# The last quarter of the attention output projection, taken into the next gated layer as seven products for each pair of tiles

## The chip, the core and the metric

The kernel runs on one core of one Trainium2 chip. A core has five engines with a queue each: TensorE (PE) for matrix products, VectorE (DVE), ScalarE (ACT), GpSimd (POOL), and SyncE (SP), which here only starts transfers. TensorE writes its results to PSUM (here in banks of 128 x 512 float32 words), from which VectorE and ScalarE read them; everything else is in SBUF. The metric is the device time of one launch in microseconds, and the median of several launches counts.

## What is computed

Four layers act in turn on x, 2048 tokens of 1024 bfloat16 values: linear attention, gated layer, and both once more with the same weights.

```python
def _A_ref(x, wqkv, wo):                     # 32 heads of 32
    q, k, v = heads of x @ wqkv
    phi = lambda t: jnp.where(t > 0, t + 1, jnp.exp(t)) + 1e-6
    pq, pk = phi(q), phi(k)
    kv = jnp.einsum("bhsd,bhse->bhde", pk, v)
    z = jnp.einsum("bhsd->bhd", pk)
    num = jnp.einsum("bhqd,bhde->bhqe", pq, kv)
    den = jnp.einsum("bhqd,bhd->bhq", pq, z)[..., None] + 1e-6
    return (num / den) @ wo
def _B_ref(x, W_gate, W_up, W_down):         # 1024 -> 3584 -> 1024
    gate, up = x @ W_gate, x @ W_up
    return (gate * (gate > 0) * up) @ W_down
x = x + _A_ref(_layernorm(x), wqkv, wo)
x = x + _B_ref(_layernorm(x), W_gate, W_up, W_down)
x = x + _A_ref(_layernorm(x), wqkv, wo)
x = x + _B_ref(_layernorm(x), W_gate, W_up, W_down)
```

## The kernel before

**Tiles.** The 2048 tokens are 16 tiles of 128 (x0 to x15), four tiles are a quarter (`sc` or `q`, 0 to 3), and the first eight tiles are the "first half" (`NS` = 8). x stays in SBUF as float32. Layers 0 and 2 are attention (`layer_A`), layers 1 and 3 are gated (`layer_B`).

**Attention, second part.** When the sums over all tokens are there, the product of the keys and values is multiplied into the output weights (`fold_wo`), which gives two slots T of 128 x 4 x 1024 in bfloat16. The output of a tile is then `out_unit` (lines 627 to 639): for each half of 512 columns, eight matmuls of the tile's transposed queries `pqT` by T, and one VectorE addition of the PSUM bank onto x (line 638). Before that, each tile's queries go through `z_mult`, `z_sum` and `z_scale` (lines 586 to 605; POOL, VectorE, POOL) and a DMA transpose into `pqT`. `out0` are the eight units of quarter 0, column by column; the loop of line 709 then runs eight units each for the quarters 1, 2 and 3, tile by tile.

**Norms for the gated layer.** `ln_later` and `ln_at` set four steps for a tile: `ln_norm` (two BATCH_NORM_STATS and one aggregate on VectorE, then Ln and Exp on ScalarE), the scaled copy `xnb` in float16 on ScalarE (line 188), a DMA transpose into `xnT` on SP's queue (line 352), and, for each pair of tiles, four VectorE sums `sums_x` (lines 796 to 799). Before the change the tiles 0 to 3 are normed while quarter 1's units run, and the tiles 4 to 7 while quarter 2's run; quarter 3's eight units come last, ahead of the first gated unit.

**The gated layer.** `glu` (line 807) does one of 14 units `u` for each half of the tokens (`c` = 0, 1). It uses Strassen's scheme in Winograd's form: a product of two by two blocks takes seven block products, not eight. For the gate (`g`) and the up projection (`u`) each there are products 5, 1, 2, 6, 7, 3, 4 of four matmuls, 56 in a unit. Products 5, 6, 7 and 3 use `sums_x`; products 4, 5, 6 and 7 use sums of weights (`make_gu`, lines 757 to 760), which VectorE makes in the first half of layer 1 and which are stored for later (`tg`, `tu`). Banks are read and then accumulated onto: `zg` (line 854) must have read `yg` before product 7 adds to it, and line 857 must have read it before product 4 does. The results are `put` (line 834) into h. `down` follows.

**Order.** `_Later` holds tasks that are due after so many ticks; every out unit and every product of a `glu` is one tick. In the attention's second part VectorE's and POOL's instructions run in the order in which they are written (`manual_schedule`, line 688); elsewhere a planner with its own model of durations orders each engine's queue ahead of time. `behind` and `issue_after` keep an instruction from being taken ahead of a given one. All large tiles share one pool of 16 slots of 8 KB per partition (`big`, line 113): T, pqT, xnT, the sums, h, the `wd` tiles, and the ring of weights, which is five deep (line 123). PSUM is split in four banks "a" (`ps`), two "b" (`ps3`) and two `kv` banks.

## Time and profile before

| what | value |
|---|---|
| median of 4 runs | 1470.31 us (1470.23 to 1470.77) |
| the profiled run's own time | 1470.4 us |
| its span, first to last instruction | 1468.6 us |
| granted TensorE clock | 1.000 |
| VectorE, ScalarE, POOL busy | 839.1, 551.9 and 285.2 us |
| VectorE instructions of line 638 (addition of an out unit) | 64, mean 667 ns |
| two BATCH_NORM_STATS of a tile, one aggregate | 671 ns each, 202 ns |
| ScalarE: Ln, Exp, scaled copy of 128 x 1024 | 290, 200 and 1238 ns |
| ScalarE: copy of a bank | 582 to 597 ns |

The span is what the profile covers; 1.8 us of the run's time lie outside it. "Idle before" in a row of the profile is the time for which the engine stood still ahead of these instructions, with what ended it behind the arrow. In the timeline, start and duration are in us from the start of the span, and successive instructions of one kind are merged (x4). [...]

### The profile page before, as it was taken

The page shows a single profiled execution, that of the slowest core. Times are in us where ns is not written, and L with a number is a line of the kernel's source. Part 1 is how long each engine was busy: PE and PEld are TensorE (multiplying, and loading weights), DVE is VectorE, ACT ScalarE, POOL GpSimd, SP SyncE. Part 2 cuts the span into 40 slices and gives each one's busy share as a digit, 9 for nine tenths or more (in the row PEclk, how much of TensorE's full clock was granted, in tenths as well). Part 3 has the DMA queues.
Part 4 walks back from the last instruction along what each step waited for, and adds up shares of the span by engine and source line. Part 5 has one row for each costly group of instructions (what it writes and reads, how often), then busy time and mean ns, then how long its engine had stood idle before and what let it go on. Part 6 is the DMA issues. An engine that isn't in the chain of part 4 may idle for free.

```text
span 1468.6 us, 18622 instructions
## 1 busy us (share of the span) xinstructions
PE 1460.4 (99%) x6937; PEld 664.3 (45%) x6975; DVE 839.1 (57%) x1475; ACT 551.9 (38%) x967; POOL 285.2 (19%) x190
## 2 busy tenths in 40 slices
PE   9999999999999999999999999999999999999999
PEld 4444444444444444444444444444444444444444
DVE  7968697666584444455368565974445434333632
ACT  6872533333340333340067625343333203333200
POOL 1444850111100011110024476301110001111000
PEclk9999999999999999999999999999999999999999
DMA  9940789556459944446743029984444688444461
GB/s 283 240 151 13 184 185 262 174 192 204 161 170 256 347 154 143 144 137 195 253 96 72 1 36 282 252 262 144 143 144 151 182 255 253 146 147 150 150 202 43
DMA packets 318363, 255.51 MB, mean 174 GB/s; under 512 B 105792, under 2 KB 291392, under 8 KB 317376
## 3 DMA queue, kind: packets, MB, share of 16 engines
q1 hardware_dynamic: 308304, 234.00, 54.7%
q10 hardware_dynamic: 9968, 20.32, 3.7%
q8 instruction: 54, 0.88, 0.3%
q14 instruction: 37, 0.30, 0.1%
HBM read 195.04 MB, written 34.60 MB: 156 GB/s over the span
## 4 chain that ended last, share of the span: by engine, by line
PE 98%; DVE 1%; issue 0%; ACT 0%; DMA 0%; DVEq 0%
PE ps L428 15%; PE yg L823 10%; PE yu L823 10%; PE dy L907 10%; PE dv L907 7%; PE dx L907 7%; PE xu L823 6%; PE xg L823 6%; PE ps L631 6%; PE vg L823 3%; PE vu L823 3%; PE zu L823 3%; PE zg L823 3%; PE my L511 3%; PE mv L511 2%; PE mx L511 2%
## 5 line engine op out<-in xcount | busy, mean ns | idle before, releaser
L823 PEld LDWEIGHTS <-w 128*128 128x128 f16 (+1 forms) x3136 | 306.5, 98 | 371.2 <-DVE w L757 0.9
L861 POOL TENSOR_TENSOR h<-m5u,m5g 128x512 f16<-128x512 f32 x56 | 71.1, 1270 | 809.7 <-DVE m5u L857 798.8
L428 PE MATMUL ps<-w,xnT 128*128 128x512 bf16 x1024 | 223.5, 379 | 0.2 <-ACT xnT L296 0.2
L907 PEld LDWEIGHTS <-h 128*128 128x128 f16 x1120 | 109.6, 98 | 132.1
L428 PEld LDWEIGHTS <-xnT 128*128 128x128 bf16 x1024 | 99.4, 98 | 120.0 <-issue 1.6
L854 DVE TENSOR_TENSOR zg<-yg,m5g 128x512 f32<-128x512 f32 x56 | 39.2, 699 | 197.5 <-PE yg L823 197.5
L823 PE MATMUL xu<-xnT,w 128*128 128x512 f16 x448 | 115.3, 379 | 0.0
L823 PE MATMUL xg<-xnT,w 128*128 128x512 f16 x448 | 115.1, 379 | 0.0
L823 PE MATMUL yu<-s,w 128*128 128x512 f16 x448 | 115.0, 379 | 0.0
L823 PE MATMUL yg<-s,w 128*128 128x512 f16 x448 | 115.0, 379 | 0.0
L631 PE MATMUL ps<-T,pqT 128*128 128x512 bf16 x500 | 110.5, 379 | 0.6
L831 ACT ACTIVATE m5g<-m5g 128x512 f32<-128x512 f32 x56 | 35.2, 629 | 199.7 <-DVE m5g L857 196.3
L907 PE MATMUL dy<-w,h 128*128 128x512 f16 x448 | 98.0, 379 | 0.0
L907 PE MATMUL dx<-w,h 128*128 128x512 bf16 x436 | 96.7, 379 | 0.6
L375 ACT ACTIVATE e<-e,eps 128x512 f32<-128x512 f32 x128 | 92.4, 722 | 4.1
L374 ACT ACTIVATE e<-ps 128x512 f32<-128x512 f32 x128 | 75.9, 593 | 45.1 <-PE ps L428 43.8
L588 POOL TENSOR_TENSOR kvc<-pq,kvc 128x1024 f32<-128x1024 bf16 x32 | 73.5, 2297 | 62.4 <-DVE den L593 38.4
L154 DVE BATCH_NORM_STATS2 stats<-x 128x6 f32<-128x512 f32 (+1 forms) x120 | 76.6, 671 | 3.0 <-DMA x<-in_A_x_dram 2.8
L161 ACT ACTIVATE rstd<-mv,eps 128x1 f32<-128x1 f32 x64 | 18.3, 290 | 159.4 <-DVE mv L159 159.2
L631 PEld LDWEIGHTS <-pqT 128*128 128x128 bf16 x512 | 49.9, 98 | 60.4 <-issue 0.5
L447 POOL TENSOR_TENSOR kvc<-kvc,slab 128x512 f32<-128x512 f32 x46 | 58.5, 1279 | 74.3 <-DVE slab L378 59.3
L834 DVE TENSOR_TENSOR h<-yu,r 128x512 f16<-128x512 f32 x56 | 38.7, 691 | 56.1 <-PE yu L823 56.1
(123 smaller groups left out, 1872.0 us busy)
## 6 DMA issues: line engine op xcount, KB each, us to landing
w<-in_B_W_gate_dram SPq DMA_DIRECT2D x56, 512.0 KB, 5.8
w<-in_B_W_up_dram SPq DMA_DIRECT2D x56, 512.0 KB, 4.8
w<-td SPq DMA_DIRECT2D x32, 896.0 KB, 4.8
w<-in_B_W_down_dram SPq DMA_DIRECT2D x24, 896.0 KB, 5.2
w<-tg SPq DMA_DIRECT2D x42, 512.0 KB, 6.9
w<-tu SPq DMA_DIRECT2D x42, 512.0 KB, 6.3
w<-in_A_wqkv_dram SPq DMA_DIRECT2D x10, 1024.0 KB, 7.1
away<-x SPq DMA_DIRECT2D x16, 512.0 KB, 4.3
```

The lines of the kernel that those rows point to most:

```text
L154: self.nc.vector.bn_stats(out=stats[:, c, :], in_=src[:, c * fmax:(c + 1) * fmax])
L374: nc.scalar.activation(out=e, in_=ps, func=ACT.Relu, scale=-1.0)
L375: nc.scalar.activation(out=e, in_=e, func=ACT.Exp, scale=-1.0, bias=self.eps6[:, 0:1])
L428: nc.tensor.matmul(by_row(ps), lhsT=self.xnT[l, l_q][:, kt, j * P:(j + 1) * P], rhs=w[:, kt, :].rearrange("p (b i d) -> p i b d", i=R, d=H ...
L447: nc.gpsimd.tensor_tensor(out=ksum[:, cols], in0=ksum[:, cols], in1=pk, op=ALU.add)
L511: nc.tensor.matmul(banks[j], lhsT=A(i)[:, j * P:(j + 1) * P], rhs=B(i), start=start and i == 0, stop=i == NS - 1, skip_group_check=True)
L588: nc.gpsimd.tensor_tensor(out=prod, in0=pq_of[sc, j], in1=zrow, op=ALU.mult)
L631: nc.tensor.matmul(ps, lhsT=pqT[sc][:, g, j * P:(j + 1) * P], rhs=T[g // 4][:, g % 4, n2 * NW:(n2 + 1) * NW], start=(g == 0), stop=(g == G ...
L823: nc.tensor.matmul(ps, lhsT=W[w][m][:, k, :], rhs=A[m][:, k, :], start=start and k == 0, stop=k == 3, skip_group_check=True)
L854: nc.vector.tensor_tensor(out=Z[w], in0=Y[w], in1=V[w], op=ALU.add)
L861: nc.gpsimd.tensor_tensor(out=h[:, 3, :], in0=V["u"], in1=V["g"], op=ALU.mult)
L907: nc.tensor.matmul(banks[j], lhsT=A(k)[:, j * P:(j + 1) * P], rhs=w[:, i, :], start=start and k == 0, stop=k == self.U - 1, skip_group_che ...
```

## The change

1. The loop over the quarters in `layer_A` ends at quarter 2. The 64 matmuls of quarter 3's units are replaced by `out_pairs`, which returns three functions for the gated layer: `sums_T` (four VectorE sums of 128 x 4 x 512 over T; in layer 0 also eight ScalarE copies that widen x12 to x15), `sums_q` (four VectorE sums of 128 x 4 x 256 over `pqT`), and `products` (seven products for two pairs of tiles each, four matmuls per pair and product, with two ScalarE copies and twelve VectorE additions). They are called in the first half of the gated layer: the sums during units 1 and 2, the products after unit 2.
2. The tiles of the first half are normed from sums: the addition of an out unit becomes a scalar_tensor_tensor with an accumulator output, and `ln_norm_sums` takes mean and variance from these sums and a ScalarE Square with an accumulator output. The norms start at once when a tile is done, and `sums_x` follows within quarter 2; `make_gu` of unit 0 in layer 1 is done there too.
3. The first unit of each gated layer takes the products 1 and 2, which need no sums, ahead of 5 and 6.
4. The loads and sums of `wd` start two units later.
5. The attention sums are scaled by 2^-11, so that the sums over T fit float16; `z_sum`, `z_row` and `finish_kv` get the factor, and the copy in `finish_kv` becomes a tensor_scalar.

```diff
@@ -172,6 +174,8 @@
     def ln_norm(self, layer, t):
 
         nc = self.nc
+        if layer % 2 and t < self.NS:
+            return self.ln_norm_sums(layer, t)
         src = self.xb[t] if layer == 0 else self.x[t]
         stats = self.small.tile([P, 2, nc.vector.BN_STATS_DIM], F32, tag="stats")
         for c in range(2):
@@ -185,6 +189,28 @@
             shift = self.small.tile([P, 1], F32, tag="shift")
             nc.vector.tensor_scalar(out=shift, in0=mv[:, 0:1], scalar1=rstd[:, 0:1], scalar2=-1.0,
                                     op0=ALU.mult, op1=ALU.mult)
+            nc.scalar.activation(out=xn, in_=src, func=ACT.Identity, scale=rstd[:, 0:1],
+                                 bias=shift[:, 0:1])
+            return xn
+
+        return scale
+
+    def ln_norm_sums(self, layer, t):
+
+        nc, src, acc = self.nc, self.x[t], self.acc[layer]
+        mv = self.small.tile([P, nc.vector.BN_AGGR_DIM], F32, tag="mv")
+        rstd = self.small.tile([P, 1], F32, tag="rstd")
+        shift = self.small.tile([P, 1], F32, tag="shift")
+        mean, ssq = mv[:, 0:1], mv[:, 1:2]
+        nc.vector.tensor_scalar(out=mean, in0=acc[:, 2 * t:2 * t + 1], scalar1=acc[:, 2 * t + 1:2 * t + 2],
+                                scalar2=-1.0 / self.D, op0=ALU.add, op1=ALU.mult)
+        xn = self.temp([P, self.D], F16, name="xnb")
+        nc.scalar.activation(out=xn, in_=src, func=ACT.Square, bias=mean, accum_out=ssq)
+        nc.scalar.activation(out=rstd, in_=ssq, func=ACT.Ln, scale=1.0 / self.D, bias=self.eps5[:, 0:1])
+        nc.scalar.activation(out=rstd, in_=rstd, func=ACT.Exp, scale=-0.5)
+
+        def scale():
+            nc.scalar.activation(out=shift, in_=mean, func=ACT.Identity, scale=rstd[:, 0:1])
             nc.scalar.activation(out=xn, in_=src, func=ACT.Identity, scale=rstd[:, 0:1],
                                  bias=shift[:, 0:1])
             return xn
...
@@ -563,9 +590,10 @@
 
         def finish_kv():
             n = NW // P
-            nc.vector.tensor_copy(out=kvT[:, 0:n, :].rearrange("p g e -> p (g e)"), in_=kv[0])
+            nc.vector.tensor_scalar(out=kvT[:, 0:n, :].rearrange("p g e -> p (g e)"), in0=kv[0],
+                                    scalar1=self.mean, scalar2=None, op0=ALU.mult)
             nc.scalar.activation(out=kvT[:, n:2 * n, :].rearrange("p g e -> p (g e)"), in_=kv[1],
-                                 func=ACT.Copy)
+                                 func=ACT.Copy, scale=self.mean)
 
 
         def q_unit(sc, j, c, lag=None):
...
@@ -635,9 +663,77 @@
             xs = self.x[t][:, cols]
 
 
-            self.last_x = nc.vector.tensor_tensor(out=xs, in0=self.xb[t][:, cols] if l == 0 else xs,
-                                                  in1=ps, op=ALU.add)
-
+            x0 = self.xb[t][:, cols] if l == 0 else xs
+            if t < self.NS:
+                if last_ln not in self.acc:
+                    self.acc[last_ln] = self.const.tile([P, 2 * self.NS], F32, name=f"acc{last_ln}")
+                self.last_x = nc.vector.scalar_tensor_tensor(
+                    out=xs, in0=ps, scalar=0.0, in1=x0, op0=ALU.add, op1=ALU.add,
+                    accum_out=self.acc[last_ln][:, 2 * t + n2:2 * t + n2 + 1])
+            else:
+                self.last_x = nc.vector.tensor_tensor(out=xs, in0=x0, in1=ps, op=ALU.add)
+
+
+        def out_pairs(sc):
+
+
+            nc, P2 = self.nc, 2 * P
+            f16 = lambda a: a.bitcast(F16)
+            b11, b12, b21, b22 = (t[:, :, n * NW:(n + 1) * NW] for t in T for n in range(2))
+            S = {}
+
+            def sums_T():
+                W = self.slot(f"sT{l}", [P, 2, 4, NW], F16)
+                S["R"] = R = self.slot(f"sR{l}", [P, 2, 4, NW], F16)
+                S[1], S[2], S[4] = W[:, 0], W[:, 1], R[:, 0]
+                op(S[1], b12, b11)
+                op(f16(b12), b22, b12)
+                op(S[2], b22, S[1])
+                op(S[4], b21, S[2])
+                if l == 0:
+                    with self.tc.issue_after(self.last_relu.ins):
+                        for t in range(sc * QT, sc * QT + QT):
+                            for n in range(2):
+                                nc.scalar.activation(out=half(self.x[t], n), in_=half(self.xb[t], n),
+                                                     func=ACT.Copy)
+
+            def sums_q():
+                q = pqT[sc]
+                a11, a12, a21, a22 = (q[:, h:h + 4, i * P2:(i + 1) * P2] for i in range(2) for h in (0, 4))
+                s1 = self.temp([P, 4, P2], F16, name="s1")
+                s2, s4 = (S["R"][:, 1, i * 2:i * 2 + 2, :].rearrange("p a (b n) -> p (a b) n", n=P2)
+                          for i in range(2))
+                op(s1, a21, a22, ALU.add)
+                op(s2, s1, a11)
+                op(f16(a21), a11, a21)
+                op(s4, a12, s2)
+                S["A"] = {1: a11, 2: a12, 3: s4, 4: a22, 5: s1, 6: s2, 7: f16(a21)}
+                S["B"] = {1: b11, 2: b21, 3: b22, 4: S[4], 5: S[1], 6: S[2], 7: f16(b12)}
+
+            def products():
+                X = [self.ps.tile([P, NW], F32, tag="a", name=f"ox{i}") for i in range(2)]
+                V = [self.ps.tile([P, NW], F32, tag="a", name=f"ov{i}") for i in range(2)]
+                Y = [self.ps3.tile([P, NW], F32, tag="b", name=f"oy{i}") for i in range(2)]
+
+                def onto(i, n, bank):
+                    xs = half(self.x[sc * QT + i], n)
+                    nc.vector.tensor_tensor(out=xs, in0=xs, in1=bank, op=ALU.add)
+
+                for m, bank, start, n in ((1, X, True, None), (5, V, True, (2, 1)), (6, Y, False, (0, 1)),
+                                          (2, X, False, (0, 0)), (7, Y, False, (2, 1)),
+                                          (3, V, False, (0, 1)), (4, Y, False, (2, 0))):
+                    for i in range(2):
+                        for k in range(4):
+                            nc.tensor.matmul(bank[i], lhsT=S["A"][m][:, k, i * P:(i + 1) * P],
+                                             rhs=S["B"][m][:, k, :], start=start and k == 0,
+                                             stop=k == 3, skip_group_check=True)
+                        if n is None:
+                            nc.scalar.activation(out=Y[i], in_=X[i], func=ACT.Copy)
+                        else:
+                            onto(n[0] + i, n[1], bank[i])
+                        later.tick()
+
+            return sums_T, sums_q, products
 
         def column_major(f, q):
             return [lambda j=j, c=c: f(q, j, c) for c in range(H) for j in range(QT)]
@@ -705,17 +801,18 @@
             ring.free_slowly((l, "o0"), later, 2)
             for i in range(11, self.ST):
                 later.at(1 + 3 * (i - 11), lambda i=i: z_mult(*divmod(i, QT)))
+            self.ln_later(last_ln, 0, 2, 2, 2)
             run(out0[3:])
-            for sc in range(1, self.NQ):
-                if sc < 3:
-                    self.ln_later(last_ln, sc - 1, 0, 3, 2)
-                if sc == 2:
+            for sc in range(1, self.NQ - 1):
+                if sc == 1:
                     for j in range(QT):
-                        later.at((8, 11, 13, 16)[j], lambda j=j: self.sums_x(last_ln, 0, j))
-                if sc == 3 and l == 0:
-                    for w in "gu":
-                        later.at(8, lambda w=w: self.make_gu(ring.get((last_ln, 0, w, 0)), w, 0))
+                        self.ln_at(2 * j + 2, last_ln, QT + j, 2)
+                        later.at((11, 13, 15, 16)[j], lambda j=j: self.sums_x(last_ln, 0, j))
+                if sc == 2 and l == 0:
+                    for n, w in enumerate("gu"):
+                        later.at(2 + 2 * n, lambda w=w: self.make_gu(ring.get((last_ln, 0, w, 0)), w, 0))
                 run(row_major(out_unit, sc))
+            self.pairs = out_pairs(self.NQ - 1)
 
 
     def plan_B(self, l):
@@ -828,30 +925,45 @@
         V, X, Y, Z, R = {}, {}, {}, {}, {}
 
         def relu(out, ps):
-            nc.scalar.activation(out=out, in_=ps, func=ACT.Relu)
+            self.last_relu = nc.scalar.activation(out=out, in_=ps, func=ACT.Relu)
 
         def put(b, ps):
             self.last_put = nc.vector.tensor_tensor(out=h[:, b, :], in0=ps, in1=R.pop(b), op=ALU.mult)
 
-        for w in "gu":
+        def five(w):
             v = self.kvp.tile([P, NW], F32, tag="kv0" if w == "g" else "kv1", name=f"v{w}")
             mm(w, 5, v, True)
             V[w] = self.temp(name=f"m5{w}")
             nc.scalar.activation(out=V[w], in_=v, func=ACT.Copy)
+
+        def one(w):
             X[w] = self.ps.tile([P, NW], F32, tag="a", name=f"x{w}")
             mm(w, 1, X[w], True)
             Y[w] = self.ps3.tile([P, NW], F32, tag="b", name=f"y{w}")
             nc.scalar.activation(out=Y[w], in_=X[w], func=ACT.Copy)
-        for w in "gu":
+
+        def two(w):
             mm(w, 2, X[w])
             if w == "g":
                 R[0] = self.temp(name="r0")
                 relu(R[0], X[w])
             else:
                 put(0, X[w])
+
+        def six(w):
             mm(w, 6, Y[w])
             Z[w] = self.ps.tile([P, NW], F32, tag="a", name=f"z{w}")
             nc.vector.tensor_tensor(out=Z[w], in0=Y[w], in1=V[w], op=ALU.add)
+
+        if c == 0 and u == 0:
+            for f in (one, two, five, six):
+                for w in "gu":
+                    f(w)
+        else:
+            for f, f2 in ((five, one), (two, six)):
+                for w in "gu":
+                    f(w)
+                    f2(w)
         for w in "gu":
             mm(w, 7, Y[w])
             nc.vector.tensor_tensor(out=V[w], in0=Y[w], in1=V[w], op=ALU.add)
@@ -958,13 +1070,17 @@
                     if u + 1 < self.U:
                         self.later.at(4, lambda u=u: behind(self.last_put if u else self.last_x, lambda: [
                             self.make_gu(ring.get((l, c, w, u + 1)), w, u + 1) for w in "gu"]))
-                    if u in (1, 5):
-                        d = self.U - 4 + u // 2
+                    if u in (3, 7):
+                        d = self.U - 4 + u // 4 * 2
                         wd[d] = self.load_d(d)
-                    if 1 < u < 10:
-                        self.later.at(4, lambda d=self.U - 4 + (u - 2) // 4 * 2, n=(u - 2) % 4: behind(
+                    if 3 < u < 12:
+                        self.later.at(4, lambda d=self.U - 4 + (u - 4) // 4 * 2, n=(u - 4) % 4: behind(
                             self.last_put, lambda: self.sums_d(wd[d], d, (n,))))
+                if c == 0 and u in (1, 2):
+                    self.later.at(6, lambda u=u: behind(self.last_put, self.pairs[u - 1]))
                 self.glu(l, c, u, hT)
+                if c == 0 and u == 2:
+                    self.pairs[2]()
                 if c == 0 and u == (self.U - 1 if first else 0):
                     after = self.last_put.ins
             if c == 0:
```

More of the change, by code (lines that the diff above doesn't have):

```diff
@@ L134, in __init__ @@
         nc.vector.memset(self.ones, 1.0)
+        self.mean = 2.0 ** -11
+        assert self.S == 2 ** 11
         self.eps6 = self.const.tile([P, 1], F32, name="eps6")
@@ L141, in __init__ @@
         self.xb = [x[:, D // 2:D].bitcast(BF16) for x in self.x]
-        self.xnT, self.xn, self.pk, self.slabs, self.xs = {}, {}, {}, {}, {}
+        self.xnT, self.xn, self.pk, self.slabs, self.xs, self.acc = {}, {}, {}, {}, {}, {}
         self.away = [self.spill.tile([P, D], F32, name=f"away{t}") for t in range(self.ST)]
@@ L456, in z_row @@
                                  start=True, stop=True)
-                nc.scalar.activation(out=zrow[:, i * NW:(i + 1) * NW], in_=ps, func=ACT.Copy)
+                nc.scalar.activation(out=zrow[:, i * NW:(i + 1) * NW], in_=ps, func=ACT.Copy,
+                                     scale=self.mean)
         def kv_half(d, mt, b):
@@ L593, in z_sum @@
             nc.vector.tensor_reduce(out=den, in_=heads(prod), axis=mybir.AxisListType.X, op=ALU.add)
-            nc.vector.tensor_scalar(out=den, in0=den, scalar1=1e-6, scalar2=None, op0=ALU.add)
+            nc.vector.tensor_scalar(out=den, in0=den, scalar1=1e-6 * self.mean, scalar2=None, op0=ALU.add)
             nc.vector.reciprocal(out=den, in_=den)
```

## The prediction

> **What bounds the kernel now.** I read the busy times first, then the chain that ended last, then the instruction groups for what TensorE waited for, and then the timeline of the two handovers from attention to the gated layer.
>
> ```profile
> PE   9999999999999999999999999999999999999999
> 422.56 12.09 PE dv L907 x56
> 434.64 24.17 PE dy L907 x112
> L823 PEld LDWEIGHTS <-w 128*128 128x128 f16 (+1 forms) x3136 | 306.5, 98 | 371.2 <-DVE w L757 0.9 <-issue 0.6 <-DVE s L796 0.5
> ```
>
> TensorE is busy in every slice (1460.4 of 1468.6 us), and PE makes up 98% of the chain. In that chain 56 matmuls of 512 columns follow one another in 12.09 us and 112 in 24.17: 0.2159 us each. So time is the number of matmuls times 0.2159 us, plus the places where TensorE stands still. The last row shows what of these lies in the gated layers: the idle time ascribed to VectorE's sums is 0.9 us (weight sums, line 757) and 0.5 us (`sums_x`, line 796). By the timeline they are at 231 to 235 us (layer 1 begins) and at 958 us (layer 3 begins).
>
> ```profile
> 232.79 1.03 PE L823 MATMUL yg<-s,w 128*128 128x512 f16 x4
> 233.87 1.03 PE L823 MATMUL vu<-s,w 128*128 128x512 f16 x4
> 234.80 1.04 PE L823 MATMUL yu<-s,w 128*128 128x512 f16 x4
> 235.67 0.81 PE L823 MATMUL vg<-s,w 128*128 128x512 f16 x3
> 233.11 1.29 DVE L757 TENSOR_TENSOR w<-w 128x1024 f16<-128x1024 bf16 x2
> 234.32 0.76 DVE L759 TENSOR_TENSOR w<-w 128x512 f16<-128x512 bf16 x2
> 234.99 0.76 DVE L760 TENSOR_TENSOR w<-w 128x512 f16<-128x512 bf16 x2
> 235.66 0.69 DVE L854 TENSOR_TENSOR zg<-yg,m5g 128x512 f32<-128x512 f32 x1
> ```
>
> Product 6 of the gate (`yg<-s`) is done at 233.8 us, but its addition `zg` runs at 235.66: VectorE first did the weight sums of the next unit, which are written earlier and were ready. `zg` is 1.8 us late, and yet TensorE hardly stood still: the queue had product 5 of the next unit (`vg` at 235.67) in between. So ready work that is written earlier goes first, and lateness of up to a few products is hidden by the next unit's.
>
> **What is saved.** Seven products of two tiles of four matmuls are 56 in place of 4 x 2 x 8 = 64. Eight fewer per attention layer, 16 in all: 16 x 0.2159 = 3.45 us. Their shape is that of the rows above, and mixed float16 and bfloat16 inputs already run at that rate in line 823.
>
> The 1.4 us of waits: weight sums of unit 0 in layer 1 are now made among quarter 2's units, and products 1 and 2 (16 matmuls, 3.45 us) go ahead of the first sums. I expect 0.9 us of the 1.4 back; ends 0 and 1.4.
>
> **The lost cover.** 64 matmuls, 13.8 us, no longer stand between the norms and the gated layer. In layer 0 an out unit takes 1.727 us and the old first gated matmul is at 228.42, so the new one is at 214.6 and the unit that ends tile 7 (8 units earlier) at 200.8. The new chain behind it:
> - The addition with its accumulator: 0.7 us like line 378, the only scalar_tensor_tensor row (681 ns); mean 0.2. A z_sum (1211 + 326 + 353 ns, 1.8 us from start to start) stands ahead of it: to 202.4 us.
> - Square as long as the scaled copy, 1.24, Ln 0.29, Exp 0.20, shift 0.2, copy 1.24: 3.2 us, to 205.6. A tile comes every 3.45 us, so ScalarE keeps up; it has no other work between 177.5 and 214.6.
> - Transpose: 3.2 to 4.6 us to landing in this stage, so some 210.
> - VectorE from 202.7 on, in written order, with start-to-start costs from the timeline (addition 0.61, weight sums 1.3 a tile, `sums_x` 1.44): 8 additions 4.9, one z_sum 1.8, two weight sums 2.6, four `sums_x` 5.8, in all 15.1 us for a 13.8 us stretch. The last `sums_x` starts at some 217.5.
>
> Product 5 wants it at 214.6 + 3.45 = 218.0. Cost zero, margin 0.1 us at the first of the four sums; if VectorE is a microsecond later, TensorE waits that long. The banks hold: an out unit takes the bank of four units before, which VectorE frees 2 us ahead.
>
> In layer 2 there are no weight sums, so VectorE has 12.5 us of work in 13.8, but the transfers are dense:
>
> ```profile
> 943.40:957.20 13.80, 13.75 (x65) 6.26 (x65) 11.12 (x27) 3.48 (x6) 0.00 (x0) 1.00 1.08 226
> 942.98 6.20 SPq L352 DMA_TRANSPOSE xnT<-xnb x4
> 947.34 0.43 DVE L796 TENSOR_TENSOR s<-xnT 128x512 f16<-128x512 f16 x1 [2.45 <-DMA xnT<-xnb]
> ```
>
> The share of the transfer engines (last but one column) is 1.08 there: full. A transpose takes 1.55 us of the queue, a 512 KB tile of x that is brought back 1.3 us (two in 2.6). From 915 us, when tile 0 is normed, up to the transpose of tile 7 lie eight of xnT, three to four of pqT and six to eight tiles of x: 25.4 to 29.6 us. So tile 7 lands at 942 to 947 us, and product 5 wants its sums at 943.4 + 3.45 = 946.8. I take 0.3 us of wait; ends 0 and 2.
>
> **The added accumulators.** Line 638 takes 667 ns, line 378 681: 14 ns more for each of 32 additions. The accumulator itself has no row; bounds are 0 and the 192 ns of a 128 x 1 tensor_scalar (line 186), so 0 to 3 us a layer, in a stretch of 22 us in which VectorE has 16 us of work. I take nothing; without that cover it would push the last `sums_x`. [...] In return 16 tiles lose two BATCH_NORM_STATS and an aggregate each: 16 x 1.5 = 24 us off VectorE, 9 us in each old handover.
>
> **The added sums and additions.** From 0.61 us for 1024 float16 elements and 0.34 for 512, start to start, 2048 take 1.15: `sums_T` is 4.6 us, `sums_q` 2.4, the twelve additions 8.3 at 0.69. A unit takes 12.09 us, of which VectorE is busy 8.0 to 8.8 in layer 1 (windows from 240 us on). Units 1 and 2 and the products, 36.3 us in all, have to hold 2 x 8.4 + 4.6 + 2.4 + 8.3 = 32.1 us: it fits on average. In unit 1 of layer 1 the order is the last `put` (to 0.9 us), weight sums (2.6), `sums_T` (4.6), then `zg`, which is due at 5.4 and runs at 8.1 to 8.8. Product 7 would start at 6.9; two products 5 and one product 1 of unit 2 can be put between (2.6 us), so it is wanted at 9.5. No wait if the planner does so, 1.9 us if not. In unit 2 `zg` is 0.5 us late at most, within the 1.7 us of two products. Between the products a bank is read and then accumulated onto one product (1.73 us) later, and an addition ends 0.9 us after its matmuls: no wait unless a weight sum of 0.61 us comes in twice. In layer 3 there are no weight sums: `sums_T` ends at 5.5, about when `zg` is due. Together I take 0.4 us; ends 0 and 4.
>
> **Other moved steps.** The eight widening copies in layer 0, 8 x 0.6 = 4.8 us of ScalarE, delay two relus by up to 1.6 us whose readers are not due (5 us idle per unit). Scaling by 2^-11 changes no instruction's size. Queries of quarter 3 (z chain to 211 us) gain 25 us. `wd` is shifted by two units, with its DMAs on SP's queue, and is stored before unit 13. Of the 16 slots, at unit 2: 2 xnT, 2 sums, 2 h, 2 T, 1 pqT, 2 new sums, 5 weights: exactly 16. The weights of unit 3 wait for those of unit 1, and then have 12.1 us of unit 2 and 12.1 of the products; they take 5.8 us, or 13.2 with their stored sums. Nothing.
>
> **Sum.** -3.45 - 0.9 + 0.3 + 0.4 = -3.65 us on the span of 1468.6; with the 1.8 us outside, and from the profiled 1470.4 (0.1 from the median), 1466.7 us. Range of this case: 1465.5 (all 1.4 back, no wait) to 1467.4.
>
> **Rivals.**
> - The waits eat the gain (0.22): layer 3 begins on late transposes (2 us) and `zg` waits in unit 1 of layer 1 (1.9), with 0.9 back: 1470.3 - 3.45 - 0.9 + 3.9 = 1469.9; with half of these waits 1467.9. For it: full transfers, 15.1 us of work in 13.8. Against: products 1 and 2 go first, and the 235.67 row.
> - Slots (0.10): if two more slots are live in unit 2 than I count, unit 3's weights load only behind the products: 5.8 us and 2.6 us of sums in layer 1, 13.2 in layer 3, against no cover: +21.6 - 4.35 gives 1487.6. It is slower by over 0.2% as soon as the two waits pass 7.3 us. Against: the `wd` tiles, which took slots from unit 1 on, now come from unit 3 on.
> - Square needs another function table (0.05). The trace has one ACT_TABLE_LOAD of 1283 ns; two per tile make ScalarE 5.8 us a tile for 3.45 us spacing, tile 7 is 19 us late, and less 8 us of margin 11 us are waited per layer: 1470.3 - 3.45 + 22 = 1489. [...] No run here shows Square.
> - The matmuls saved, and nothing else (within the main case): 1466.9.
>
> **Chances.** Main case 0.63, of which 0.03 end above 1467.4. 0.2%, 2.9 us, is about what a measurement of this kernel can tell from no change; the border is 1467.4. Faster 0.60, within 0.24 (0.21 of the first rival and the main case's edge), slower 0.16 (the next two, and 0.01 of the first). Range: 1465.4 to 1470.4, which leaves out the slower rivals and little more.
>
> **What would show it.** Right: of line 631's 512 matmuls 384 left and 112 new ones; first gated matmul near 214.6 us with no wait on `s` or `w`; `zg` of unit 1 in layer 1 late by 2 to 3 us with another product in TensorE's row at that point. Wrong: idle time of PE's weight loads ahead of product 5 in layer 3 by a DMA, gaps around the twelve additions, an ACT_TABLE_LOAD beyond the first, or unit 3 waiting for `w`.

## The result and the profile after

| | median us | range, runs | span of the profiled run |
|---|---|---|---|
| before | 1470.79 | 1470.19 to 1473.65, 53 | 1468.6 |
| after | 1472.78 | 1471.11 to 1476.36, 33 | 1471.7 |

The ratio is 1.0013 [1.0008, 1.0018]: the change costs 0.13%, where 0.25% less was forecast. The profiled execution took 1473.47 us, 0.7 above its median, at a granted clock of 0.999.

I read the time where it is set, in TensorE's row. Matmuls of 512 columns start 0.216 us apart (their records, 379 ns each, overlap); what is above that is time lost. The table sums this excess, in us, over the spacings of matmul starts that are more than 20 ns too long, by stage (where the trace lacks a matmul, a spacing of two, 0.432 us, is not counted):

| stage (us from the start) | before | after |
|---|---|---|
| to 180 (start, layer 0's first part and fold) | 4.01 | 4.15 |
| 180 to 300 (handover of layer 0 to 1, units 0 to 2, products) | 0.57 | 2.77 |
| 300 to 912 (rest of layer 1, layer 2 up to its fold) | 1.07 | 1.07 |
| 912 to 1020 (handover of layer 2 to 3, units 0 to 2, products) | 0.19 | 4.45 |
| 1020 to the end | 0.0 | 0.0 |

Sixteen matmuls fewer are there (weight loads 6975 before, 6959 after): -3.45 us. The two handovers lose 2.20 and 4.26 us more than before. With 0.14 us in the first stage this makes the 3.1 us by which the span grew.

The larger loss first. These are rows of the timeline of after (start, duration, engine, line, operation, count, and in brackets the idle time before and what ended it): TensorE, then VectorE, then SyncE's queue.

```profile
946.53 1.03 PE L920 MATMUL xu<-xnT,w 128*128 128x512 f16 x4
949.93 1.86 PE L920 MATMUL vg<-s,w 128*128 128x512 f16 x4 [2.38 <-DVE s L893]
951.59 1.76 PE L920 MATMUL vu<-s,w 128*128 128x512 f16 x4
953.18 1.03 PE L920 MATMUL yg<-s,w 128*128 128x512 f16 x4
...
947.29 0.42 DVE L893 TENSOR_TENSOR s<-xnT 128x512 f16<-128x512 f16 x1 [2.86 <-DMA xnT<-xnb]
...
936.28 3.44 SPq L378 DMA_TRANSPOSE xnT<-xnb  x2
939.78 1.06 SPq L256 DMA_DIRECT2D x<-away  x2
940.94 1.23 SPq L633 DMA_TRANSPOSE pqT<-pq  x1
942.27 4.35 SPq L378 DMA_TRANSPOSE xnT<-xnb  x2
```

The reader is to follow it upwards: product 5 (`vg`) stands for the last `sums_x`, VectorE stands 2.86 us for the last transpose, and that transpose was started only at 942.27, behind two tiles x brought back and a transpose of `pqT` (939.78 and 940.94), which were ready earlier and stand ahead of it in the queue. Then four matmuls take 1.86 us rather than 1.03. The view of stretches tells why (length, PE, PEld, DVE, ACT and POOL busy, granted clock, share of the transfer engines, GB/s):

```profile
944.00:947.00 3.00, 3.00 (x16) 1.35 (x15) 0.43 (x1) 1.44 (x3) 0.00 (x0) 1.00 1.17 251
950.00:953.00 3.00, 3.00 (x8) 1.05 (x9) 1.51 (x4) 0.60 (x1) 0.00 (x0) 0.50 0.97 328
```

The granted clock is 0.50 after the pause, and in 3 us 7 matmuls start (an eighth is still under way) in place of 14. So the wait costs 2.5 us and the half rate after it 1.5 (eight spacings of up to 0.427 us). The half rate isn't in every execution: of the 33, 14 have a granted clock of 0.999, which fits one such stretch (3.41 us at 0.50 take 0.001 off the mean of 1471.7 us), and take 1473.12 us or more; the other 19 have 1.000 and take 1473.11 us or less.

The handover of layer 0, TensorE and then VectorE and GpSimd:

```profile
216.95 1.02 PE L920 MATMUL xu<-xnT,w 128*128 128x512 f16 x4 [1.04 <-DVE x L674]
...
219.95 1.04 PE L920 MATMUL vg<-s,w 128*128 128x512 f16 x4 [0.25 <-DVE s L893]
...
224.71 1.02 PE L920 MATMUL yg<-s,w 128*128 128x512 f16 x4 [0.27 <-DVE zg L956]
...
207.59 2.01 DVE L856 TENSOR_TENSOR w<-w 128x512 f16<-128x512 bf16 x1
...
213.35 0.42 DVE L856 TENSOR_TENSOR w<-w 128x512 f16<-128x512 bf16 x1
...
207.15 2.16 POOL L628 TENSOR_TENSOR pq<-pq,den 128x1024 bf16<-128x1024 bf16 x1 [1.83 <-DVE den L623]
```

Three waits: for a bank that VectorE has not read yet (1.2 us by spacing), of product 5 for the sums (0.42), and for `zg` (0.43). The spacing of the weight loads gives 0.63 us at product 5, but the next load then follows after 0.015 us; the expectations below use that reading. In unit 1 product 7 waits for `zg` again (0.36 us), in unit 2 for `zu` (0.22). The same weight sum takes 0.42 us at 213.35 and 2.01 us at 207.59, where GpSimd's last scaling of queries (207.15 to 209.31) runs.

### The profile page after: what moved, and what is told of

It is laid out like the page before. It is cut to its first block, busy times and chain, and to the rows that moved or that the text cites. A ratio compares the mean times of both kernels' runs of the same rounds, so it can differ in the third digit from the quotient of the medians.

```text
span 1471.7 us, 18656 instructions
## 1 busy us (share of the span) xinstructions
PE 1458.9 (99%) x6920; PEld 663.2 (45%) x6959; DVE 842.0 (57%) x1483; ACT 578.5 (39%) x1027; POOL 285.2 (19%) x190
## 4 chain that ended last, share of the span: by engine, by line
PE 94%; DVE 3%; ACT 1%; DMA 1%; issue 1%; SPq 0%; DVEq 0%; ACTq 0%
PE ps L454 15%; PE dy L1019 10%; PE yu L920 10%; PE yg L920 10%; PE dv L1019 7%; PE dx L1019 7%; PE xg L920 6%; PE xu L920 6%; PE zu L920 3%; PE zg L920 3%; PE vg L920 3%; PE vu L920 3%; PE my L538 3%; PE ps L659 3%; PE mv L538 2%; PE mx L538 2%
## 5 line engine op out<-in xcount | busy, mean ns | idle before, releaser
L659 PE MATMUL ps<-T,pqT 128*128 128x512 bf16 x374 | 83.0, 379 | 0.5
L937 ACT ACTIVATE m5g<-vg 128x512 f32<-128x512 f32 x56 | 33.4, 597 | 113.4 <-PE vg L920 87.8
L969 DVE TENSOR_TENSOR m5u<-yu,m5u 128x512 f32<-128x512 f32 x56 | 38.7, 691 | 53.6 <-PE yu L920 53.6
L1019 PEld LDWEIGHTS <-e 128*128 128x128 f16 x448 | 43.9, 98 | 52.8
```

The lines of the kernel that those rows point to most:

```text
L659: nc.tensor.matmul(ps, lhsT=pqT[sc][:, g, j * P:(j + 1) * P], rhs=T[g // 4][:, g % 4, n2 * NW:(n2 + 1) * NW], start=(g == 0), stop=(g == G ...
L1019: nc.tensor.matmul(banks[j], lhsT=A(k)[:, j * P:(j + 1) * P], rhs=w[:, i, :], start=start and k == 0, stop=k == self.U - 1, skip_group_che ...
```

## The experiments

Theory: the transfers that the change leaves in the old order on SyncE's queue stand ahead of the last transposes at layer 3, and VectorE's written order makes the waits at layer 1. Rivals: the new VectorE sums and additions themselves, the norms from sums, the matmuls' new operands. All versions below start from the kernel after; the ratio is to the kernel before, run beside it.

**1. The transfers of x12 to x15 behind the last transpose.**

```diff
-        nc.sync.dma_start_transpose(out=self.xnT[layer, q][:, :, j * P:(j + 1) * P], in_=xn)
+        self.last_xnT = nc.sync.dma_start_transpose(out=self.xnT[layer, q][:, :, j * P:(j + 1) * P], in_=xn)
...
-            for t in range(self.NS, self.ST, 2):
+            for t in (8, 10):
                 later.at(10 + t, lambda t=t: self.behind(self.last_turn, bring, (t, t + 1)))
+            for t in (12, 14):
+                later.at(16 + t, lambda t=t: self.behind(self.last_xnT, bring, (t, t + 1)))
```

> The changed kernel with one edit: the transfers of x12 to x15, which are now needed only in unit 1 or later, are put behind the last transpose of the first eight tiles on SP's queue, in both attention layers. Theory of the queue (mine): at the handover to layer 3 TensorE waits 2.7 us ahead of product 5, and the next seven matmuls take 0.427 us each in place of 0.216 (1.5 us), because the last two transposes of xnT stand in the queue behind two to four tiles of x at 1.3 us each. Then these transposes are issued 2.5 to 5 us earlier, the wait shrinks to under 0.5 us, the 0.427 us matmuls vanish with it, and the kernel comes 3 to 4.2 us below the changed one, about 1468.5 to 1469.8. Rival (norm chain): ScalarE's chain for tiles 6 and 7 ends too late (937.4 us); then the wait keeps most of its length and the time changes by less than 1 us. Rival (evictions): most of the loss is in units 1 to 3, and nothing changes.

1470.49 us, ratio 0.9998 [0.9989, 1.0006]. Timeline of this version, SyncE and TensorE:

```profile
938.25 1.29 SPq L633 DMA_TRANSPOSE pqT<-pq  x1
939.63 2.66 SPq L378 DMA_TRANSPOSE xnT<-xnb  x2
942.35 1.05 SPq L256 DMA_DIRECT2D x<-away  x2
...
947.25 1.03 PE L922 MATMUL xu<-xnT,w 128*128 128x512 f16 x4
948.11 1.03 PE L922 MATMUL vg<-s,w 128*128 128x512 f16 x4
```

The last transposes start 2.6 us earlier, product 5 follows without a gap, and the stage's excess falls from 4.45 to 0.39 us, the half-rate matmuls with it. The excess of layer 0's handover stays (2.96). So layer 3's loss was the queue's order, and the half rate went with the wait. The median is 2.3 us below that of after, less than the 3 to 4.2 expected, while the profiled executions differ by 3.3: the median execution of after has a granted clock of 1.000 and so, by that sign, no half rate, which the expectation counted in full. Of the 11 executions of this version one has 0.999.

**2. Two attempts that made it worse.** `x_pq_late` is version 1 with the `pqT` transposes of quarter 3 also put behind the last `xnT`:

```diff
+            def turn():
+                self.last_turn = nc.sync.dma_start_transpose(out=pqT[sc][:, :, j * P:(j + 1) * P], in_=pq)
+            if sc < self.NQ - 1:
+                turn()
+            else:
+                later.at(12, lambda: self.behind(self.last_xnT, lambda _: turn(), (0,)))
```

`sums0_early` is after with the weight sums of unit 0 made a quarter earlier (`if sc == 1` in place of `sc == 2`, at ticks 2 and 6); `both_handovers` has the two together.

> As the run before, and the four transposes of quarter 3's queries are also put behind those of xnT. Theory of the queue: three transposes at 1.55 us leave the queue ahead of the last two of xnT, so the last xnT lands near 941 to 943 us, ahead of product 5 at 947; no wait at all at the handover to layer 3, 3.8 to 4.5 us below the changed kernel. If x alone was enough, this run equals the one before within 0.5 us. Norm chain rival: no gain beyond the run before and a wait that stays.

> The changed kernel with one edit: the weight sums of unit 0 of layer 1 are made among quarter 1's out units in place of quarter 2's. Theory (VectorE is over full in quarter 2's stretch of layer 0): 2.6 us of VectorE work and one sum that took 2.01 us beside GpSimd leave that stretch, the wait of 1.2 us for a bank (ahead of the second matmul group of unit 0) and the 0.6 us ahead of product 5 vanish: 1.2 to 1.8 us below the changed kernel. Rival (transfers): the sums wait for transposes in layer 0 as well, and less than 0.5 us is gained.

> The edits of the two runs before together. If both handovers are the loss, their gains add: 5 to 6.3 us below the changed kernel and 3 to 4.3 us below the kernel before, near 1466.5 to 1467.8, which is the saving of 16 matmuls (3.45 us) plus the old waits (1.4) less some 1 us of waits in units 0 to 2 of layer 1. If the evictions and sums within units 1 to 3 cost the saving, it stays at or above the kernel before.

1475.21 us (1.0027 [1.0016, 1.0037]), 1475.33 (1.0032 [1.002, 1.0044]) and 1477.15 (1.0045 [1.0032, 1.0057]). All three expectations missed. In the first the delayed transposes went ahead of unit 1's weights on the same queue, VectorE stood 1.53 us for those and TensorE 1.89 for `zg`; in layer 3 they held the pool's slot which `sums_T` needs, and TensorE stood 2.15 us. In the second the weight sums fell beside other work of GpSimd: two took 1.43 and 2.44 us rather than 0.68, a third 2.02 rather than 0.42, and the banks came free too late in three places. Here each step moved off one place cost at the place where it landed.

**3. GpSimd out of the way.** Version 1, with the chain of query scalings run on at its pace up to the last tile, in place of three ticks a tile from tile 11 on:

```diff
-            if i < 10:
+            if i < 15:
                 later.at(2 + i % 2, lambda: z_chain(i + 1))
...
-            for i in range(11, self.ST):
-                later.at(1 + 3 * (i - 11), lambda i=i: z_mult(*divmod(i, QT)))
```

> x_late with one edit more: the chain that divides the queries of quarter 3 by their sums keeps its pace of 2 to 3 ticks per tile to the end, in place of 3, so that GpSimd's last scaling ends ahead of the weight sums and sums_x of quarter 2's stretch. Theory (GpSimd holds VectorE up): in layer 0 one weight sum took 2.01 us in place of 0.42 while GpSimd scaled the queries of tile 15 (207.2 to 209.3 us). Without this overlap it takes 0.42, the wait of 1.2 us for a bank in unit 0 falls below 0.4, and the kernel comes 1.0 to 1.6 us below x_late, near 1469. Rival (amount): the stretch holds 15.1 us of VectorE work in 13.8 whatever GpSimd does; then the wait stays at 0.8 us or more and less than 0.5 us is gained.

1472.13 us, 1.0006 [0.9997, 1.0015]. VectorE, GpSimd and TensorE of it:

```profile
207.22 0.43 DVE L856 TENSOR_TENSOR w<-w 128x512 f16<-128x512 bf16 x1
...
204.73 1.92 POOL L628 TENSOR_TENSOR pq<-pq,den 128x1024 bf16<-128x1024 bf16 x1 [0.57 <-DVE den L623]
...
215.86 1.03 PE L920 MATMUL xu<-xnT,w 128*128 128x512 f16 x4
...
218.45 1.03 PE L920 MATMUL vg<-s,w 128*128 128x512 f16 x4
```

The scaling now ends at 206.65, the weight sum behind it takes 0.43 us, and the waits for the bank and for product 5's sums are gone. How much of them GpSimd alone made, this version doesn't separate: measured from the first gated matmul, VectorE is through with these weight sums 2.1 us earlier, of which 0.9 are shorter sums (the one ahead took 1.35 us rather than 0.63), and the rest an earlier start, since the version moves that tile's `z_sum` on VectorE forward too. And the time is no better: TensorE now stands 2.22 us for `zg`, up to 224.29, and runs at half rate afterwards (1.7 us). VectorE had come to the weight sums of unit 1 earlier, which stand ahead of `zg` in its order, and stood 1.44 us for their weights. In layer 3 the earlier chain costs 0.8 us (excess 1.20).

**4. The order of sums on VectorE.** `sums_first` is version 3 with the four `sums_x` at ticks 11, 13, 14, 14 rather than 11, 13, 15, 16; `pairs_later` has the sums for the products at tick 9 rather than 6 as well.

> z_early with one edit more: sums_x of tiles 2 and 6 and of 3 and 7 are written ahead of the last two additions of quarter 2. Theory: product 5 of unit 0 needs these sums 3.45 us after the handover, the two banks are wanted only by the additions zg and zu later; the wait of 0.6 us ahead of product 5 in layer 1 goes: 0.4 to 0.8 us below z_early. In layer 3 the transposes land by 942 to 944 us, so that the additions behind them are late by 1 us at most, for nobody. Rival: the wait moves to the banks and nothing is gained.

> sums_first with one edit more: the sums over T and over the queries are called at the ninth tick of units 1 and 2 in place of the sixth, behind the additions zg and zu. Theory: the waits of 0.36 and 0.22 us ahead of product 7 in units 1 and 2 of layer 1 go, as zg is no longer behind 1.2 us sums: 0.3 to 0.6 us below sums_first. Rival: the sums only push later readers of banks, and it comes out within 0.3 us either way.

1472.64 us (1.0009 [1.0, 1.0017]) and 1472.88 (1.0013 [1.0004, 1.0021]): neither gains. The pause for `zg` is 2.94 and 3.08 us long: being earlier at `sums_x` only let VectorE reach the stalled weight sums sooner. The later sums for the products take the gap of unit 1 from 0.36 to 0.17 us and put 0.42 into unit 2 of layer 3.

**5. The norms from sums undone.** Version 1 with the statistics instructions back; the accumulators are still written, but not used.

```diff
-        if layer % 2 and t < self.NS:
-            return self.ln_norm_sums(layer, t)
```

> x_late with the second part of the change undone: the tiles of the first half are normed with BATCH_NORM_STATS again, while the accumulators are still written. Eight tiles get 1.5 us of VectorE work more each, 12 us in the 36 us from the end of the first column of quarter 0 to the handover, in which VectorE works 28 to 31 us and runs late at the end already. Theory: VectorE falls 4 to 8 us behind, TensorE waits for banks and for sums_x in both layers: 5 to 12 us above x_late. Rival (the new norms bring nothing, ScalarE's longer chain eats it): within 1 us of x_late.

1478.03 us, 1.0048 [1.0035, 1.0062]; the excess is 7.90 us at layer 1 and 3.53 at layer 3, against 2.96 and 0.39. The second part of the change is needed: without the 13.8 us of cover the old norms cost 7.5 us more by the medians (8.1 in the two stages), within what was expected.

**6. The weight sums of unit 1, by number of ticks.** `sums1_later` is version 1 with

```diff
-                        self.later.at(4, lambda u=u: behind(self.last_put if u else self.last_x, lambda: [
+                        self.later.at(4 if u else 9, lambda u=u: behind(self.last_put if u else self.last_x, lambda: [
```

`z0_sums1` adds version 3's chain in layer 0 alone, `z0_order_sums1` also the ticks 14, 14 of version 4 in layer 0, and `z0_order_x` brings x12 to x15 back six ticks later in layer 0 on top.

> Version x_late (1470.49 us, span 1468.3), and the weight sums of unit 1 are written to VectorE's queue at tick 9 of unit 0 instead of tick 4, in both layers, so zg of unit 0 stands ahead of them. Theory (VectorE's order, zg stands behind an addition that is not due yet): the wait of 0.43 us at 224.4 in layer 1 shrinks to 0.1, the bank wait (1.2 us at 215.8) and that at product 5 (0.63 at 219.4) stay, since they lie ahead of it: about 0.4 us less than x_late, 1470.1. Rival (the sums of unit 1 are needed as early as they stand): a new wait at product 5 of unit 1 near 227 us, 1 us or more, and the time is 1471 or above.

> x_late, the weight sums of unit 1 at tick 9, and in layer 0 alone the z chain is spread so that its last parts go with the tiles up to the last but one and GpSimd has no z_scale left when the sums are made. Theory: z_early lost its gain to a single wait of 2.22 us for zg at 224.3, behind weight sums that stood for their transfer, and to the half-rate matmuls after it (1.7 us). With the sums behind zg both go, and so does the bank wait at 215.8 (1.2 us): x_late 1470.5 - 1.2 - 0.6 - 0.4 = about 1468.3, faster than the kernel before by 0.15%. Rival (the weights of unit 1 are simply late, whoever waits): the wait moves to product 5 of unit 1, some 2 us near 227 us, and the time stays at 1471 to 1472.

> z0_sums1, and in layer 0 the last two sums of the attention tiles are written one to two tiles earlier. If the sums' place in VectorE's order still makes product 5 wait in z0_sums1, this takes the rest (up to 0.6 us): 1467.7 to 1468.3. If they wait for the transposes instead, additions of the last tiles stand behind them, TensorE waits for banks, and the time is 0.5 to 1.5 us above z0_sums1.

> z0_order_sums1, and in layer 0 the tiles x12 to x15 are brought back six ticks later, so that half of them follow the weights of unit 1 on SP's queue. If transfers of weights behind those of x are what is left (unit 1's weight sums stand for their DMA), the remaining wait near 224 to 227 us drops by 1 to 2 us against z0_order_sums1; if nothing waits for those weights any more, the time is the same within 0.3 us.

1469.96 us (0.9993 [0.9984, 1.0002]), 1471.63 (1.0009 [1.0, 1.0017]), 1471.71 (1.0006 [0.9997, 1.0015]) and 1468.46 (0.9987 [0.9978, 0.9996]). The first has the time that the theory expected, but by luck: `zg` still holds TensorE up for 0.41 us (0.64 in `x_late`), where 0.1 was expected, because VectorE still does three of unit 1's weight sums ahead of it. The middle two kept the pause for `zg` (2.45 and 2.63 us), which the theory had gone; their times are those of the rival, but the wait did not move to unit 1 as the rival had it. The last one shows why; VectorE's timeline:

```profile
219.86 0.69 DVE L856 TENSOR_TENSOR w<-w 128x1024 f16<-128x1024 bf16 x1 [0.18 <-DMA w<-in_B_W_up_dram]
220.47 0.68 DVE L933 TENSOR_TENSOR h<-xu,r 128x512 f16<-128x512 f32 x1
221.07 0.75 DVE L858 TENSOR_TENSOR w<-w 128x512 f16<-128x512 bf16 x2
221.73 0.76 DVE L859 TENSOR_TENSOR w<-w 128x512 f16<-128x512 bf16 x2
222.40 0.70 DVE L958 TENSOR_TENSOR zg<-yg,m5g 128x512 f32<-128x512 f32 x1
```

With x out of the way VectorE stands only 0.18 us for the weights, but the weight sums are still ahead of `zg`, although they are called at tick 9: the planner puts them there. A pause of 1.28 us is left. Whether the order or the late weights set it, this version alone doesn't tell.

**7. The weight sums pinned behind `zu`.**

```diff
-            nc.vector.tensor_tensor(out=Z[w], in0=Y[w], in1=V[w], op=ALU.add)
+            self.last_z = nc.vector.tensor_tensor(out=Z[w], in0=Y[w], in1=V[w], op=ALU.add)
...
-                        self.later.at(4 if u else 9, lambda u=u: behind(self.last_put if u else self.last_x, lambda: [
+                        self.later.at(4 if u else 9, lambda u=u: behind(self.last_put if u else self.last_z, lambda: [
```

`z0_order_z` has this on `z0_order_x`, `z_order` on version 1 with nothing else, and `z_order_pairs` is `z0_order_z` with `sums_T` of layer 1 pinned in the same way.

> z0_order_x (1468.46 us, span 1466.8), and the weight sums of unit 1 in layer 1 are pinned behind the last addition zu of unit 0 on VectorE. Theory (the written order): zg then runs at about 220.5 instead of 222.4, the wait of 1.28 us near 222 is gone, nothing follows it since unit 1's product 5 is due some 5 us later: 1468.46 - 1.4 = 1467.1, and the excess between 180 and 300 us falls from 1.9 to about 0.5. Rival (unit 1's weights are late, whoever waits): the wait of 1 us or more moves to product 5 of unit 1 near 227 us, and the time stays at 1468 or above.

> x_late (1470.49 us), and only the pinning of unit 1's weight sums behind zu. Theory: the wait of 0.43 us near 224.4 goes, while the bank wait (1.2 us at 215.8) and that at product 5 (0.63 at 219.4), which lie ahead of it, stay: 1470.0. Rival (the wait for zg is the main loss of layer 1, the others merely shift it): 1469.0 or less.

> z0_order_z, and sums_T in unit 1 of layer 1 is pinned behind zu of that unit. Theory: the wait of 0.36 us near 235.5 goes too, 1466.8. Rival: the sums of unit 2's and 3's weights and sums_q, now later, make a new wait in unit 2 (0.5 us or more near 240 to 250 us), and nothing is gained.

| version | median us | ratio to before | excess 180 to 300 us | 912 to 1020 us |
|---|---|---|---|---|
| x_late | 1470.49 | 0.9998 [0.9989, 1.0006] | 2.96 | 0.39 |
| z_order | 1468.87 | 0.9989 [0.9980, 0.9997] | 2.26 | 0.38 |
| z0_order_z | 1467.33 | 0.9979 [0.9970, 0.9988] | 0.50 | 0.38 |
| z_order_pairs | 1467.47 | 0.9980 [0.9971, 0.9989] | 0.50 | 0.38 |

TensorE and VectorE of `z0_order_z`:

```profile
219.52 1.03 PE L922 MATMUL vg<-s,w 128*128 128x512 f16 x4
...
222.11 1.03 PE L922 MATMUL yu<-s,w 128*128 128x512 f16 x4
223.13 1.02 PE L922 MATMUL yg<-s,w 128*128 128x512 f16 x4
...
222.38 0.70 DVE L958 TENSOR_TENSOR zg<-yg,m5g 128x512 f32<-128x512 f32 x1 [1.45 <-PE yg L922]
...
223.84 1.28 DVE L856 TENSOR_TENSOR w<-w 128x1024 f16<-128x1024 bf16 x2
```

VectorE now waits for TensorE's `yg` rather than the other way round, and unit 1 doesn't feel the weight sums at 223.84. So the order was the cause, and the weights were not late for anybody else. `z0_order_z` is faster than both kernels: 3.5 us below the 1470.86 of before beside it, what sixteen matmuls are worth. `z_order` has the time that the rival expected (1469.0 or less), but the waits that the theory expected: its layer-1 excess is 0.70 us lower than in `x_late` (the waits in units 0 to 2), while the bank's wait and product 5's are still there. The other 0.9 us between the medians lies elsewhere: the first 160 us alone, which no edit here touches, differ by 0.74 us between the two profiled runs. The wait in unit 1 that `z_order_pairs` was to remove is no longer there in `z0_order_z`, and nothing measurable was gained.

## Why the prediction was wrong

Right:
- **The saving.** Sixteen matmuls fewer, and the first gated matmul at 214.89 us (forecast 214.6). `z0_order_z`, whose two handovers lose 0.88 us where before loses 0.76, shows their 3.45 us: it is 3.5 us faster.
- **Accumulators, Square, slots.** In the trace of after the accumulator is an instruction of its own, 83 ns on VectorE (DVE_READ_ACCUMULATOR, 32 of them; bounds were 0 and 192) and 187 ns on ScalarE (ACTIVATION_READ_ACCUMULATOR, 16); Square takes 1.14 us, and there is one ACT_TABLE_LOAD (1283 ns), as in before. No product waited for a slot, and the twelve additions left no gap between the products (254 to 266 us are solid). The rivals built on these are out.
- **The sums in units 1 and 2.** `sums_T` takes 1.22 us an operation, `sums_q` 0.68; `zg` of unit 1 ran late with two products 5 in between, as told. They cost 0.36 + 0.22 us in layer 1 and 0.23 in unit 1 of layer 3, 0.8 in all where 0.4 was taken, within the ends of 0 and 4.

Wrong: the sum was -3.45 - 0.9 + 0.3 + 0.4 us; the traces show -3.45, +2.20 at layer 1 and +4.26 at layer 3.
- **"I take 0.3 us of wait; ends 0 and 2" at layer 3.** It measured 4.3 us more than before. The step was close on the transfers' total time (tile 7 was to land at 942 to 947; VectorE took it at 947.29), although its own prices (1.55 and 1.3 us a transfer) give 24.9 to 29.0 us and so 940 to 944. But it took the middle of an interval in which 1 us decided, priced a queue as a sum instead of writing down its order, and gave the wait itself as its only cost. The half-rate matmuls that followed this pause, 1.5 us in the profiled execution, were in no term. The rival "the waits eat the gain" named the place and put 2 us on it; its sum, 1469.9, was too low as well.
- **"Cost zero, margin 0.1 us" at layer 1.** It measured 0.42 us at product 5, and 1.2 us at a bank which "the banks hold" had excluded. The last `sums_x` began at 219.48 us. The step took 217.5, and its own sum, 15.1 us from 202.7 with `sums_x` of 1.44 at the end, gives 216.4. Of these 3.1 us, 1.6 are a weight sum that took 2.01 us beside GpSimd's scaling, where the sum has 0.42, as at 213.35; another 1.04 are VectorE standing for an out unit, up to 204.59, with the `z_sum` written behind it. The step had itself told that TensorE waits from a microsecond on, and yet carried no cost for it.
- **`zg` of unit 0.** It was counted for units 1 and 2 alone. The row at 235.66 of before, which I read as harmless because another product lay in between, shows the same order at work; 0.43 us here, and pauses of 1.28 to 3.08 us in the six versions in which VectorE got there sooner in the same order.
- **"I expect 0.9 us of the 1.4 back."** There was not that much to get. The 1.4 us are idle time of the weight loads, which isn't that of the matmuls: at 231.91 a load starts 0.679 us after the last one, and the next only 0.015 later, where the matmuls are 0.470 apart. By the starts of its matmuls the kernel before loses only 0.57 and 0.19 us in the two stages. In after larger waits took their place, and `z0_order_z`, with 0.50 and 0.38 us, gets nothing back either.

## What to carry to other kernels

When matmuls are taken out from between two stages, list every instruction that now has less cover, and for each queue write its order at that point, transfers included: here two tiles of x and a transpose of `pqT`, ready earlier and written earlier, went first (939.78 and 940.94 us), and the last transposes, started at 942.27, set the end. Price VectorE's work by what it takes beside the engines that run there (2.01 us for a weight sum here), not by its best row (0.42), and treat a margin of 0.1 us as a cost (0.42 us at product 5 here). A repair that brought VectorE forward sent it sooner into the next wait (`z_early`: TensorE stands 2.22 us for `zg`), so remove the waits in one go or pin the order, and judge the set rather than each.

## What was unexpected in the hardware

**Half rate after some pauses.** After pauses of 2.22 us (`z_early`), 2.38 (after), 2.45 (`z0_sums1`) and 2.94 (`sums_first`) the next matmuls came more slowly: up to 0.427 us apart in after (granted clock 0.50, in the stretch shown above), four of them in up to 1.91 us rather than 1.03 in `z_early` and `z0_sums1`, and in 1.45 us in `sums_first`. After 2.63 us (`z0_order_sums1`), 2.93 (`old_norms`) and 3.08 (`pairs_later`) they started 0.216 us apart (four in 1.02 us, eight in 1.89). TensorE's rows of `z0_sums1` and then `z0_order_sums1`, each with the row of a stretch of 3.41 us that ends in the pause or just behind it (columns as above, TensorE's busy time second):

```profile
224.48 1.79 PE L922 MATMUL yg<-s,w 128*128 128x512 f16 x4 [2.45 <-DVE zg L958]
226.06 1.91 PE L922 MATMUL zg<-s,w 128*128 128x512 f16 x4
...
221.18:224.60 3.42, 0.97 (x5) 0.39 (x4) 3.17 (x7) 0.60 (x1) 0.00 (x0) 1.00 1.16 295
```

```profile
224.75 1.02 PE L922 MATMUL yg<-s,w 128*128 128x512 f16 x4 [2.63 <-DVE zg L958]
225.61 1.03 PE L922 MATMUL zg<-s,w 128*128 128x512 f16 x4
...
220.67:224.08 3.41, 1.45 (x7) 0.58 (x6) 2.62 (x7) 0.00 (x0) 0.00 (x0) 1.00 1.17 295
```

So in these seven runs the length of the pause alone doesn't decide. Where the pause falls is one thing that differs. In after the granted clock changes at 4.15, 949.64 and 953.06 us: the half rate lasted 3.413 us, and the 945.49 us ahead of it are 277 times as long; in before the clock changes at 4.67 and 1468.99 us, 429 such steps apart. Counted by them, TensorE was idle for 2.09 us of the step ahead of the half rate in after (946.22 to 949.64 us), and for 1.04 us at most of any other step between the first 20 us and the last matmul. Of the two stretches above, each as long as a step, the first has 2.45 us of idle time, with half rate behind it; the second has 1.96 us, without, and its pause goes on for another 0.67 us. Where between 1.96 and 2.09 us a border would lie, and whether there is one, these runs don't show.

**VectorE sums beside GpSimd's scaling.** In after a weight sum took 2.01 us at 207.59, while GpSimd scaled queries (207.15 to 209.31), and the same sum 0.42 at 213.35, when GpSimd had nothing to do; in `z_early`, where the scaling ended at 206.65, it took 0.43 at 207.22. In `z_order` it took 2.01 us at 207.34, again beside the scaling (from 206.91 on). What holds the sum up there is not shown; the 1.6 us are this case's size for it.
